# Top-k attention with two expert layers on one core: products with values of two consecutive pairs of heads in one block

## The chip, the cores and the metric

The kernel runs on one core of a Trainium2 chip. The metric is the device time of one execution in microseconds, the median of several runs. Inputs, outputs and all arithmetic seen by the caller are float32.

## The reference

```python
scores = (1 / sqrt(64)) * q @ k.T             # batch 2, 8 heads, 576 rows, head size 64
kth = the 32nd largest score of each row
p = softmax(where(scores >= kth, scores, -1e9))
x = (p @ v), heads side by side               # 1152 x 512
g = domain_probs / sum(domain_probs)          # 1152 x 4
x = sum over 4 experts of g[:, e] * (relu(x @ w1[e]) @ w2[e])        # inner size 1024
out = max(x @ m1, x @ m2, x @ m3) @ mo        # inner size 768
```

## The kernel before

The 1152 rows are nine tiles of 128. A batch has 576 rows, so tile 4 is mixed: its first 64 rows belong to batch 0, the others to batch 1. The work of attention comes in 36 **pairs**: one tile and two heads (`hp`, 0 to 3). Pairs 0 to 15 are tiles 0 to 3; pairs 16 to 23 are tiles 4 and 5 in the order of `MIX`, (4,0), (5,0), (4,1), (5,1), (4,2), (4,3), (5,2), (5,3); pairs 24 to 35 are tiles 6 to 8.

A pair passes through these steps of class `Pair`. PE makes the scores of head j (`scores`, L408); ACT copies them from PSUM to `s` (L432), in buffers with the tags s0 (five of them, `AHEAD_S`) and s1 (four, `S1`). DVE finds the 32 largest of each row with four MAX8 and three MATCH_REPLACE8 (`topk`, L437). ACT and DVE make the masked exponentials `p` (`exp`, `mask`) and their sums. PE turns `p` (`trans_p`, L484): four blocks of 128 columns for each head into one bank, which ACT copies to `pt` (L494), and the 64 columns left over of both heads into another, copied to `pt4` (L499). The two `pt` of a pair have one buffer each. DVE takes the reciprocal of the sums (`rr`, L510), ACT spreads it over 64 columns for each head (`rb`, L514), PE turns that too (`trans_r`, L516, bank `psr`) and ACT copies it to `r` (L521). The product with values (`pv`, L523, bank `psv`) is one full-width matmul with the left-over rows (`v_last`, 128 columns of weights, L533) and eight half-width ones (`vt`, 64 columns of weights, head 0 into partitions 0 to 63 and head 1 into 64 to 127, L536). The matmuls are plain f32 and each appears in a trace as two records. For a mixed tile all of this is done once for each batch, on half of the columns. DVE multiplies the product by `r` into `xt` (`norm`, L540), and `split_x` (L545) makes a high part `xh` on ACT and a low part `xl` on POOL.

The experts' matmuls are f32r: each product is three of them, `xl` by `whi`, `xh` by `whi`, `xh` by `wlo` (L684 to L686). All banks but two come from one ring of six (`bank`).

The order of every engine's instructions is fixed when the program is built. Attention is laid out in slots, eight to a pair, by tables of slot numbers (`FIRST` to `LOOSE`; pairs from 12 on mostly use `BOTH` or `LOOSE`, which put the product with values and the turn of `r` at slot 17 of the pair, that is slot 1 two pairs later). After each slot the planner in the main loop adds work of the experts until a counter of PE's columns (`clock["pe"]`) has reached a goal that grows with DVE's work of that slot. An engine then takes its instructions in that order, each when its semaphores allow it.

Of the kernel before, what the change touches and what calls it, by code (L numbers as in the profile page):

```python
# [10 lines left out]
F32 = mybir.dt.float32  # L11
# [35 lines left out]
EARLY = 7  # L47

# [12 lines left out]
def kernel(  # L61
# [71 lines left out]
    def pe(n):  # L133
        clock["pe"] += n / 2400.0
# [264 lines left out]
    class Pair:  # L399
        def __init__(self, n):  # L400
            self.n = n
            self.c, self.hp, self.t = pairs[n]
            self.s, self.w, self.m, self.nb = {}, {}, {}, {}
            self.p = self.rs = None
            self.pt = {}

            self.did = set()

            self.on_pool = [n in ON_POOL[j] for j in range(2)]
            self.on_act = [n in ON_ACT[j] for j in range(2)]  # L410
# [74 lines left out]
        def trans_p(self, part):  # L485
# [3 lines left out]
            if part < 2:  # L489
                for r in range(NR):  # L490
                    nc.tensor.transpose(ps[:, r * P:(r + 1) * P], self.p[:, part, part * TAIL + r * P:part * TAIL + (r + 1) * P], ident)  # L491
                d = at.tile([P, NR, P], F32, tag="pt%d" % part, bufs=1, name="pt")
                self.pt[part] = d
                return lambda: [nc.scalar.activation(out=d, in_=ps.rearrange("p (r n) -> p r n", r=NR), func=AF.Copy),  # L494
                                self.did.add(("pt", part))]
# [16 lines left out]
        def spread(self):  # L512
            self.rb = at.tile([P, 2, D], F32, tag="rb", bufs=1, name="rb")
            nc.scalar.activation(out=self.rb, in_=self.rr.unsqueeze(2).to_broadcast([P, 2, D]), func=AF.Copy)  # L514

        def trans_r(self):  # L516
            ps = bank("psr")
            pe(260)
            nc.tensor.transpose(ps[:, 0:P], self.rb.rearrange("p a d -> p (a d)"), ident)
            self.r = at.tile([P, P], F32, tag="r", name="r")  # L520
            return lambda: [nc.scalar.activation(out=self.r, in_=ps[:, 0:P], func=AF.Copy), self.did.add("r")]  # L521

        def pv(self):  # L523
            assert {("pt", i) for i in range(3)} <= self.did
            ps = bank("psv")
            pe((NR + 1) * 512)
            if self.t == MIXED:
                parts = [(0, slice(0, TAIL)), (1, slice(TAIL, P))]
            else:
                parts = [(0 if self.t < MIXED else 1, slice(0, P))]  # L530
            for b, cols in parts:
                vs, last = vt[b, self.hp]
                nc.tensor.matmul(ps[:, cols], lhsT=last, rhs=self.pt[2][:, cols], start=True, stop=False)  # L533
                for r in range(NR):
                    for j in range(2):
                        nc.tensor.matmul(ps[j * D:(j + 1) * D, cols], lhsT=vs[:, j * NR + r, :],  # L536
                                         rhs=self.pt[j][:, r, cols], start=False, stop=r == NR - 1)
            self.x = ps

        def norm(self):  # L540
            assert "r" in self.did
            self.xt = xfull[:, self.hp, :] if [self.t] in STAGES else at.tile([P, P], F32, tag="xt", bufs=2 + WAITING, name="xt")
            nc.vector.tensor_tensor(out=self.xt, in0=self.x[:, 0:P], in1=self.r, op=ALU.mult)
# [15 lines left out]
    def attention():  # L559
# [38 lines left out]
        for n, (c, hp, t) in enumerate(pairs):  # L598
# [24 lines left out]
            at_slot(s0 + o["pv"], pr.pv)  # L623
            two(s0 + o.get("turn", o["rec"] + 2), pr.trans_r)
            end = max(o["pv"], o["rec"] + 2) + o["lag"]
            if "norm" in o:
                between.setdefault(s0 + o["norm"], []).append((pr.norm, ()))
            else:
                at_slot(s0 + end + 1, pr.norm)
            two(s0 + o.get("split", end + 2), pr.split_x)  # L630
        last = {}
        for n, p in enumerate(pairs):
            o = options(n)
# [451 lines left out]
```

## Time and profile before

| | us |
|---|---|
| median of 3 runs | 742.99 |
| lowest and highest | 742.87, 744.54 |
| the profiled execution | 743.31 |
| its span, first to last instruction | 740.8 |
| PE busy in the span | 718.4 |
| DVE, ACT, POOL busy | 582.6, 504.9, 474.2 |

The profiled execution's time is 2.5 us longer than its span: that lies before the first and after the last instruction. PE's clock is granted in full throughout (1.00 in every stretch). Attention ends at about 450 us, and what follows is the rest of the experts and the last layer. Matmuls overlap each other in the pipeline, so the time from one start to the next tells what one costs, not its duration.

### The profile page before, as it was taken

To read this page: it belongs to the slowest core of one execution; us is meant where nothing else is said; L and a number is where in the kernel's file an instruction comes from. 1 tells how busy PE (TensorE), PEld (TensorE's weight loads), DVE (VectorE), ACT (ScalarE), POOL (GpSimd) and SP (SyncE) were. 2 spreads that over 40 slices of the span, in tenths; PEclk is the share of its full clock that TensorE was granted. 3 is DMA by queue.
4 is the path that set the end of the run, shared out by engine and by line. 5 is a ranking of instruction groups with operands and counts; after the bars stand their busy time and mean duration, and the time that the engine had idled before them with its cause. 6 is when DMAs were issued, how large, how long until landed. Compare 5 with 4: busy or idle time off the path is not lost.

```text
span 740.8 us, 13773 instructions
## 1 busy us (share of the span) xinstructions
PE 718.4 (97%) x4758; PEld 641.4 (87%) x4758; DVE 582.6 (79%) x1172; ACT 504.9 (68%) x1131; POOL 474.2 (64%) x420
## 2 busy tenths in 40 slices
PE   6799999999999999999999999999999999999998
PEld 4587689888989988898998989999989999998996
DVE  6999989989999899999999983867689783333431
ACT  4668989899977878697878777656657654442531
POOL 2513879679979797777878769756645683442520
PEclk9999999999999999999999999999999999999999
DMA  7584455644646464544545537796988764443501
GB/s 220 179 261 176 135 181 168 174 118 138 202 143 189 114 192 124 169 130 129 155 126 161 154 118 241 247 320 195 310 275 308 234 190 186 160 165 109 191 1 42
DMA packets 56485, 130.15 MB, mean 176 GB/s; under 512 B 9760, under 2 KB 23328, under 8 KB 56416
## 3 DMA queue, kind: packets, MB, share of 16 engines
q1 hardware_dynamic: 48064, 120.69, 52.1%
q10 hardware_dynamic: 8352, 8.59, 3.3%
q8 instruction: 37, 0.61, 0.3%
q14 instruction: 32, 0.26, 0.1%
HBM read 120.60 MB, written 8.65 MB: 174 GB/s over the span
## 4 chain that ended last, share of the span: by engine, by line
PE 69%; DVE 15%; ACT 9%; issue 3%; POOL 2%; DMA 1%; ACTq 0%; POOLq 0%
PE ps L684 17%; PE ps L686 17%; PE ps L685 17%; DVE m L445 7%; DVE work L447 6%; PE psv L536 3%; ACT whi L273 3%; PE pss L425 2%; PE psp L491 2%; POOL wlo L279 2%; PE pso L684 2%; PE psa L769 2%; PE pso L685 2%; PE pso L686 2%; PE pss L420 1%
## 5 line engine op out<-in xcount | busy, mean ns | idle before, releaser
L279 POOL TENSOR_TENSOR wlo<-raw,whi 128x512 fp32r<-128x512 f32 x252 | 327.6, 1329 | 130.1 <-ACT whi L273 122.8
L273 ACT ACTIVATE whi<-raw 128x1024 fp32r<-128x1024 f32 x164 | 170.1, 1057 | 36.5 <-PE ps L686 17.0
L684 PE MATMUL ps<-xl,whi 128*128 128x256 f32 (+1 forms) x584 | 173.5, 297 | 0.4 <-POOL xl L557 0.4
L686 PE MATMUL ps<-xh,wlo 128*128 128x256 f32 (+1 forms) x584 | 170.7, 292 | 0.0
L685 PE MATMUL ps<-xh,whi 128*128 128x256 f32 (+1 forms) x584 | 170.6, 292 | 0.0
L445 DVE MAX8 m<-work 128x8 f32<-128x576 f32 x216 | 155.1, 744 | 0.1
L684 PEld LDWEIGHTS ps<-xl,whi 128*128 128x128 f32 x584 | 110.7, 190 | 1.4 <-POOL xl L557 0.6
L685 PEld LDWEIGHTS ps<-xh,whi 128*128 128x128 f32 x584 | 109.7, 188 | 0.8 <-issue 0.2
L686 PEld LDWEIGHTS ps<-xh,wlo 128*128 128x128 f32 x584 | 109.6, 188 | 0.0
L279 DVE TENSOR_TENSOR wlo<-raw,whi 128x1024 fp32r<-128x1024 f32 x38 | 55.7, 1468 | 68.6 <-ACT whi L273 56.7
L447 DVE MATCH_REPLACE8 work<-m,work 128x576 f32<-128x576 f32 x144 | 106.7, 741 | 0.0
L684 PE MATMUL ps<-wlo,h 128*128 128x512 f32 x224 | 90.8, 405 | 0.6 <-POOL wlo L279 0.6
L686 PE MATMUL ps<-whi,h 128*128 128x512 f32 x224 | 87.8, 392 | 1.3 <-POOL h L821 1.3
L685 PE MATMUL ps<-whi,h 128*128 128x512 f32 x224 | 87.7, 391 | 0.0
L249 POOL TENSOR_TENSOR narrow<-narrow,raw 128x256 int32<-128x256 int32 x48 | 45.0, 940 | 30.7 <-issue 10.2
L432 ACT ACTIVATE s<-pss 128x288 f32<-128x288 f32 x144 | 51.2, 399 | 11.6 <-PE pss L420 11.2
L445 DVE MAX8 m<-s 128x8 f32<-128x576 f32 x72 | 53.8, 747 | 4.5 <-ACT s L432 4.5
L447 DVE MATCH_REPLACE8 work<-m,s 128x576 f32<-128x576 f32 x72 | 53.4, 741 | 0.0
L686 PEld LDWEIGHTS ps<-whi,h 128*128 128x128 f32 x224 | 42.1, 188 | 11.2 <-POOL h L821 1.7
L684 PEld LDWEIGHTS ps<-wlo,h 128*128 128x128 f32 x224 | 42.9, 192 | 8.2 <-POOL wlo L279 1.6
L686 PE MATMUL ps<-x2h,wlo 128*128 128x384 f32 x144 | 48.5, 337 | 0.0
L685 PE MATMUL ps<-x2h,whi 128*128 128x384 f32 x144 | 48.3, 336 | 0.0
(111 smaller groups left out, 1461.2 us busy)
## 6 DMA issues: line engine op xcount, KB each, us to landing
raw<-in_w_dram SPq DMA_DIRECT2D x128, 512.0 KB, 4.1
raw<-narrow SPq DMA_DIRECT2D x36, 512.0 KB, 4.4
raw<-in_m_dram SPq DMA_DIRECT2D x36, 256.0 KB, 5.1
whole<-in_w_dram SPq DMA_DIRECT2D x14, 512.0 KB, 6.2
narrow<-narrow ACTq DMA_DIRECT2D x48, 128.0 KB, 4.4
kraw<-in_k_dram SPq DMA_DIRECT2D x16, 288.0 KB, 4.5
qraw<-in_q_dram SPq DMA_DIRECT2D x48, 64.0 KB, 3.9
raw<-in_mo_dram SPq DMA_DIRECT2D x12, 256.0 KB, 4.7
```

The lines of the kernel that those rows point to most:

```text
L249: nc.gpsimd.tensor_tensor(out=out.bitcast(I32), in0=out.bitcast(I32), in1=last, op=ALU.add)
L273: nc.scalar.activation(out=hi, in_=raw, func=AF.Copy)
L279: on.tensor_tensor(out=lo[:, x], in0=raw[:, x], in1=hi[:, x].bitcast(F32), op=ALU.subtract)
L425: nc.tensor.matmul(ps[:, 0:SH], lhsT=l, rhs=r, start=i == 0, stop=i == len(mm) - 1)
L432: nc.scalar.activation(out=s[:, h, :], in_=halves[h][:, 0:SH], func=AF.Copy)
L445: nc.vector.max(m[:, 8 * r:8 * r + 8], src)
L447: nc.vector.match_replace(out=self.w[j], in_to_replace=m[:, 8 * r:8 * r + 8], in_values=src, imm_value=NEG)
L491: nc.tensor.transpose(ps[:, r * P:(r + 1) * P], self.p[:, part, part * TAIL + r * P:part * TAIL + (r + 1) * P], ident)
L536: nc.tensor.matmul(ps[j * D:(j + 1) * D, cols], lhsT=vs[:, j * NR + r, :], rhs=self.pt[j][:, r, cols], start=False, stop=r == NR - 1)
L684: nc.tensor.matmul(ps, lhsT=lh, rhs=rl, start=first, stop=False)
L685: nc.tensor.matmul(ps, lhsT=lh, rhs=rh, start=False, stop=False)
L686: nc.tensor.matmul(ps, lhsT=ll, rhs=rh, start=False, stop=last)
```

## The change

For twelve pairs (`HELD`) the product with values is not made at the pair's own slot. The pair after it makes both: `pv` puts the two results side by side in one bank, first all matmuls with `v_last` and then all half-width ones, and `trans_r` turns both `rb` into one bank, from which ACT makes two copies. With the two pairs of each couple that is 24 pairs. Until then the held pair's `pt` lie in a buffer of `s0` and one of `s1`, and its `rb` in one of `xt`'s. `norm` and `split_x` of both pairs follow each other at the second one's slots.

```diff
--- before.py
+++ after.py
@@ -45,6 +45,7 @@
 LOOSE = dict(stag=4, new=1, scores=-4, at=(14, 14), pv=17, rec=15, lag=2, sum=0)
 
 EARLY = 7
+HELD = (8, 12, 14, 16, 18, 22, 24, 26, 28, 30, 32, 34)
 
 ALONE_FROM, ALONE_STEP = -8, 4
 LOAD, LOAD_FULL = 11, 9
@@ -405,6 +406,7 @@
             self.pt = {}
 
             self.did = set()
+            self.held = n in HELD
 
             self.on_pool = [n in ON_POOL[j] for j in range(2)]
             self.on_act = [n in ON_ACT[j] for j in range(2)]
@@ -489,7 +491,10 @@
             if part < 2:
                 for r in range(NR):
                     nc.tensor.transpose(ps[:, r * P:(r + 1) * P], self.p[:, part, part * TAIL + r * P:part * TAIL + (r + 1) * P], ident)
-                d = at.tile([P, NR, P], F32, tag="pt%d" % part, bufs=1, name="pt")
+                if self.held:
+                    d = at.tile([P, NR, P], F32, tag="s%d" % part, bufs=(AHEAD_S, S1)[part], name="pt")
+                else:
+                    d = at.tile([P, NR, P], F32, tag="pt%d" % part, bufs=1, name="pt")
                 self.pt[part] = d
                 return lambda: [nc.scalar.activation(out=d, in_=ps.rearrange("p (r n) -> p r n", r=NR), func=AF.Copy),
                                 self.did.add(("pt", part))]
@@ -510,37 +515,49 @@
             nc.vector.reciprocal(out=self.rr, in_=self.rs)
 
         def spread(self):
-            self.rb = at.tile([P, 2, D], F32, tag="rb", bufs=1, name="rb")
+            self.rb = at.tile([P, 2, D], F32, tag="xt", bufs=2 + WAITING, name="rb") if self.held else at.tile([P, 2, D], F32, tag="rb", bufs=1, name="rb")
             nc.scalar.activation(out=self.rb, in_=self.rr.unsqueeze(2).to_broadcast([P, 2, D]), func=AF.Copy)
 
-        def trans_r(self):
+        def trans_r(self, *held):
+            both = [*held, self]
             ps = bank("psr")
-            pe(260)
-            nc.tensor.transpose(ps[:, 0:P], self.rb.rearrange("p a d -> p (a d)"), ident)
-            self.r = at.tile([P, P], F32, tag="r", name="r")
-            return lambda: [nc.scalar.activation(out=self.r, in_=ps[:, 0:P], func=AF.Copy), self.did.add("r")]
-
-        def pv(self):
-            assert {("pt", i) for i in range(3)} <= self.did
+            for i, x in enumerate(both):
+                pe(260)
+                nc.tensor.transpose(ps[:, i * P:(i + 1) * P], x.rb.rearrange("p a d -> p (a d)"), ident)
+                x.r = at.tile([P, P], F32, tag="r", name="r")
+
+            def copy():
+                for i, x in enumerate(both):
+                    nc.scalar.activation(out=x.r, in_=ps[:, i * P:(i + 1) * P], func=AF.Copy)
+                    x.did.add("r")
+            return copy
+
+        def pv(self, *held):
+
+            both = [*held, self]
             ps = bank("psv")
-            pe((NR + 1) * 512)
-            if self.t == MIXED:
-                parts = [(0, slice(0, TAIL)), (1, slice(TAIL, P))]
-            else:
-                parts = [(0 if self.t < MIXED else 1, slice(0, P))]
-            for b, cols in parts:
-                vs, last = vt[b, self.hp]
-                nc.tensor.matmul(ps[:, cols], lhsT=last, rhs=self.pt[2][:, cols], start=True, stop=False)
+            for i, x in enumerate(both):
+                assert {("pt", a) for a in range(3)} <= x.did
+                x.x = ps[:, i * P:(i + 1) * P]
+            pe((NR + 1) * 512 * len(both))
+            uses = []
+            for x in both:
+                if x.t == MIXED:
+                    uses += [(x, 0, slice(0, TAIL)), (x, 1, slice(TAIL, P))]
+                else:
+                    uses += [(x, 0 if x.t < MIXED else 1, slice(0, P))]
+            for i, (x, b, cols) in enumerate(uses):
+                nc.tensor.matmul(x.x[:, cols], lhsT=vt[b, x.hp][1], rhs=x.pt[2][:, cols], start=not i, stop=False)
+            for i, (x, b, cols) in enumerate(uses):
                 for r in range(NR):
                     for j in range(2):
-                        nc.tensor.matmul(ps[j * D:(j + 1) * D, cols], lhsT=vs[:, j * NR + r, :],
-                                         rhs=self.pt[j][:, r, cols], start=False, stop=r == NR - 1)
-            self.x = ps
+                        nc.tensor.matmul(x.x[j * D:(j + 1) * D, cols], lhsT=vt[b, x.hp][0][:, j * NR + r, :],
+                                         rhs=x.pt[j][:, r, cols], start=False, stop=i == len(uses) - 1 and r == NR - 1)
 
         def norm(self):
             assert "r" in self.did
             self.xt = xfull[:, self.hp, :] if [self.t] in STAGES else at.tile([P, P], F32, tag="xt", bufs=2 + WAITING, name="xt")
-            nc.vector.tensor_tensor(out=self.xt, in0=self.x[:, 0:P], in1=self.r, op=ALU.mult)
+            nc.vector.tensor_tensor(out=self.xt, in0=self.x, in1=self.r, op=ALU.mult)
 
         def split_x(self):
             if not room(self.t):
@@ -620,16 +637,21 @@
             at_slot(s0 + o.get("guard", o["rec"] - 1), pr.guard)
             at_slot(s0 + o["rec"], pr.recip)
             at_slot(s0 + o.get("spread", o["rec"] + 1), pr.spread)
-            at_slot(s0 + o["pv"], pr.pv)
-            two(s0 + o.get("turn", o["rec"] + 2), pr.trans_r)
+            if pr.held:
+                continue
+            both = [prs[n - 1], pr] if n - 1 in HELD else [pr]
+            at_slot(s0 + o["pv"], pr.pv, *both[:-1])
+            two(s0 + o.get("turn", o["rec"] + 2), pr.trans_r, *both[:-1])
             end = max(o["pv"], o["rec"] + 2) + o["lag"]
-            if "norm" in o:
-                between.setdefault(s0 + o["norm"], []).append((pr.norm, ()))
-            else:
-                at_slot(s0 + end + 1, pr.norm)
-            two(s0 + o.get("split", end + 2), pr.split_x)
+            for x in both:
+                if "norm" in o:
+                    between.setdefault(s0 + o["norm"], []).append((x.norm, ()))
+                else:
+                    at_slot(s0 + end + 1, x.norm)
+                two(s0 + o.get("split", end + 2), x.split_x)
         last = {}
         for n, p in enumerate(pairs):
+            n += n in HELD
             o = options(n)
             last[p[0:2]] = 8 * n + o.get("last", max(o["pv"], o["rec"] + 2) + 2 * o["lag"] + 2)
         for n in range(len(alone)):
```

The instructions are the same in kind and number on every engine; the order changes. On PE, the products with values of pair 26 (at `v_last_111`) and pair 27 (`v_last_112`) before; `pt_`, `ps_` with a number are the left-over rows of turned p and a bank of the experts' products:

```order
L686 MATMUL ps_4685<-xh,wlo 128x256
L533 MATMUL psv<-pt_4672,v_last_111 128x128
L536 MATMUL psv<-pt,vt 64x128 x8
L519 MATMUL psr<-ident,rb 128x128
L684 MATMUL ps_4763<-wlo,h 128x512
L685 MATMUL ps_4763<-whi,h 128x512
L686 MATMUL ps_4763<-whi,h 128x512
```

A block of one pair stands alone among the experts' f32r products, with its one turn of `rb` behind it. Pair 27, later on PE:

```order
L686 MATMUL ps_4860<-xh,wlo 128x256
L533 MATMUL psv<-pt_4836,v_last_112 128x128
L536 MATMUL psv<-pt,vt 64x128 x8
L519 MATMUL psr<-ident,rb 128x128
L684 MATMUL ps_4941<-xl,whi 128x256
L685 MATMUL ps_4941<-xh,whi 128x256
L686 MATMUL ps_4941<-xh,wlo 128x256
```

The two blocks are 61 rows apart. In the changed kernel both stand at pair 27's place on PE:

```order
L706 MATMUL ps_4880<-xl,whi 128x256
L707 MATMUL ps_4880<-xh,whi 128x256
L708 MATMUL ps_4880<-xh,wlo 128x256
L550 MATMUL psv<-pt_4657,v_last_111 128x128
L550 MATMUL psv<-pt_4833,v_last_112 128x128
L554 MATMUL psv<-pt,vt 64x128 x16
L526 MATMUL psr<-ident,rb 128x128 x2
L706 MATMUL ps_4880<-xl,whi 128x256
```

The two `v_last` matmuls come first, 16 half-width ones follow, and then two turns; at pair 26's old place the experts' products run on.

ACT about the copy of `r` for pair 27 before (`s`: scores, `whi`: a weight's high part, `h`: a hidden layer's, `rs`: the sums):

```order
L432 ACTIVATE s<-pss 128x288 x2
L273 ACTIVATE whi<-raw 128x1024
L826 ACTIVATE h<-ps_4860 128x512
L521 ACTIVATE r<-psr 128x128
L273 ACTIVATE whi<-raw 128x1024
L556 ACTIVATE xh<-xt 128x128
```

And in the changed kernel, for pairs 26 and 27:

```order
L434 ACTIVATE s<-pss 128x288 x2
L531 ACTIVATE r<-psr 128x128 x2
L274 ACTIVATE whi<-raw 128x1024
L573 ACTIVATE xh<-xt 128x128 x2
L848 ACTIVATE h<-ps_4880 128x512
L509 ACTIVATE rs<-rs 128x2
```

The two copies of `r` follow each other directly behind the copies of scores; the rounding of a weight and of a hidden layer, which stood ahead of `r`, come behind it. The two `xh` follow each other too.

## Rows read from the trace of the kernel before

**Rows 1.** the page: span and busy time of each engine

```profile
span 740.8 us, 13773 instructions
...
PE 718.4 (97%) x4758; PEld 641.4 (87%) x4758; DVE 582.6 (79%) x1172; ACT 504.9 (68%) x1131; POOL 474.2 (64%) x420
```

**Rows 2.** the chain of waits, 330 to 345 us: start us, us, what

```profile
332.18 1.33 DVE m L445 x2
...
339.41 0.53 PE pss L425 x2
```

**Rows 3.** the chain by line, 341 to 450 us

```profile
by line: PE ps L684 24.0%; PE ps L686 23.9%; PE ps L685 23.9%; PE psv L536 9.1%; PE psp L491 7.2%; PE pss L425 6.8%; PE psv L533 2.1%; PE psr L519 2.1%; PE psp L496 1.0%
```

**Rows 4.** the chain by line, 450 to 741 us

```profile
by line: PE ps L684 28.2%; PE ps L686 28.1%; PE ps L685 28.0%; PE pso L684 4.3%; PE pso L685 4.3%; PE pso L686 4.2%; PE pst L905 1.4%; PE psv L536 0.2%; DVE ob L975 0.1%; ACT ob L973 0.1%; PE psr L519 0.1%; issue 0.0%
```

**Rows 5.** busy time by stretch: PE, PEld, DVE, ACT, POOL, then clock, DMA

```profile
160.00:240.00 80.00, 78.79 (x611) 71.77 (x610) 79.56 (x166) 69.13 (x165) 72.41 (x64) 1.00 0.57 168
...
258.00:340.00 82.00, 79.68 (x621) 71.99 (x621) 78.73 (x168) 65.20 (x159) 67.23 (x60) 1.00 0.52 154
340.00:450.00 110.00, 110.00 (x838) 99.47 (x838) 100.31 (x215) 88.41 (x208) 82.84 (x73) 1.00 0.46 137
```

**Rows 6.** PE's timeline about pair 15's products: start us, us, what

```profile
201.15 0.38 PE L533 MATMUL psv<-pt,v_last 128*128 128x128 f32 x2
201.47 1.09 PE L536 MATMUL psv<-pt,vt 128*64 128x128 f32 x16
202.49 0.33 PE L519 MATMUL psr<-ident,rb 128*128 128x128 f32 x1
202.57 0.36 PE L684 MATMUL ps<-xl,whi 128*128 128x256 f32 x1
202.78 0.28 PE L685 MATMUL ps<-xh,whi 128*128 128x256 f32 x1
202.90 0.28 PE L686 MATMUL ps<-xh,wlo 128*128 128x256 f32 x1
```

**Rows 7.** the same, a window that begins at 201.86 us

```profile
201.63 0.82 PE L536 MATMUL psv<-pt,vt 128*64 128x128 f32 x12
```

**Rows 8.** the same, a window that begins at 202.28 us

```profile
202.06 0.50 PE L536 MATMUL psv<-pt,vt 128*64 128x128 f32 x6
```

**Rows 9.** PE's timeline, the mixed pair 16

```profile
212.75 0.33 PE L533 MATMUL psv<-pt,v_last 128*128 128x64 f32 x2
213.01 0.69 PE L536 MATMUL psv<-pt,vt 128*64 128x64 f32 x16
213.63 0.43 PE L533 MATMUL psv<-pt,v_last 128*128 128x64 f32 x2
213.99 0.69 PE L536 MATMUL psv<-pt,vt 128*64 128x64 f32 x16
214.61 0.33 PE L519 MATMUL psr<-ident,rb 128*128 128x128 f32 x1
```

**Rows 10.** PE's timeline, turning pair 28's p

```profile
362.06 1.04 PE L491 MATMUL psp<-ident,p 128*128 128x128 f32 x8
362.93 0.27 PE L496 MATMUL psp<-ident,p 128*128 128x128 f32 x1
```

**Rows 11.** PE's timeline, pair 24: its wait in brackets

```profile
314.56 0.49 PE L533 MATMUL psv<-pt,v_last 128*128 128x128 f32 x2 [1.19 <-ACT pt L499]
```

**Rows 12.** DVE's timeline after that wait

```profile
322.78 0.69 DVE L828 SCALAR_TENSOR_TENSOR h<-ps,h 128x512 fp32r<-128x512 f32 x1 [1.14 <-ACT h L826]
```

**Rows 13.** DVE's timeline, pair 28's p

```profile
354.50 0.81 DVE L473 SCALAR_TENSOR_TENSOR p<-s,m,p 128x576 f32<-128x576 f32 x1
```

**Rows 14.** ACT's timeline, the last copy of pair 19's p

```profile
250.02 0.28 ACT L499 ACTIVATE pt<-psp 128x128 f32<-128x128 f32 x1
```

**Rows 15.** PE's timeline, pair 19's products

```profile
250.85 0.38 PE L533 MATMUL psv<-pt,v_last 128*128 128x128 f32 x2
```

**Rows 16.** ACT's timeline, the copy of pair 15's r

```profile
203.83 0.28 ACT L521 ACTIVATE r<-psr 128x128 f32<-128x128 f32 x1
```

## The prediction

> **What bounds the kernel now.** I read the page first: PE is busy for 718.4 of the span's 740.8 us [rows 1]. A busy PE is an average, so I went to the chain of waits, stretch by stretch. From 341 to 450 us every piece of it is PE's [rows 3], and from 450 us to the end all but the last copy out is PE's too [rows 4]. Just before that the chain still passes through DVE (332 us), and comes back to PE at 339.4 us [rows 2]. So a PE instruction that goes away after 339 us shortens the run by its whole length, as long as nothing else is late next. The table by stretch tells where something else is: from 160 to 240 us DVE is busy for 79.56 of 80 us, so there PE has nothing to gain by being quick. From 258 to 340 us DVE is idle for 82.00 - 78.73 = 3.3 us and from 340 to 450 us for 110.00 - 100.31 = 9.7 us [rows 5]. A piece of that idle time is DVE's wait for a hidden layer that PE finished late [rows 12], so there DVE can follow a quicker PE.
>
> **How far PE is behind DVE.** What DVE hands to PE is p. Pair 28's p is written by 354.50 + 0.81 = 355.3 us [rows 13], and PE turns it at 362.06 us [rows 10]: 6.7 us to spare. The tight place is the other one, the product with values, which needs ACT's copy of the turned p. Pair 19's last copy ends at 250.02 + 0.28 = 250.30 us [rows 14], and PE begins at 250.85 us [rows 15]: 0.55 us to spare.
>
> **What one joined product saves.** No instruction is added or removed; the counts on all five engines stay. What goes is time between matmuls. A single block, pair 15's [rows 6], in start-to-start times:
> - Its two full-width records (v_last) take 201.47 - 201.15 = 0.32 us. Eight records of full-width f32 transposes stand 362.93 - 362.06 = 0.87 us apart, 0.11 each [rows 10], so two should take 0.22. The other 0.10 us is the change to half-width matmuls.
> - Its 16 half-width records start two by two, in eight steps, and take 202.49 - 201.47 = 1.02 us. In the middle, one window shows twelve records from 201.63 us on [rows 7] and a later one the six from 202.06 us on [rows 8]: so four steps take 0.43 us, 0.11 each. Eight of them make 0.87, so the two ends cost 0.15 us.
> - The turn of r stands 0.08 us before the next product, which itself stands 202.78 - 202.57 = 0.21 us before its successor, where 202.90 - 202.78 = 0.12 us is usual. Leaving costs 0.09 us.
>
> Two blocks joined pay these once: 0.10 + 0.15 + 0.09 = 0.34 us saved. The second turn of r now follows another turn, 0.11 us against 0.08, so 0.31 us remain for each couple.
>
> Two of the twelve couples hold a mixed pair, 16 and 18. Its two batches are two full blocks today [rows 9]: the second one takes 213.99 - 213.63 = 0.36 and 214.61 - 213.99 = 0.62, together 0.98 us. With half the columns a v_last record should take half of 0.11. The eight steps of the first, 213.63 - 213.01 = 0.62 us, are 0.15 of ends and 0.47 of work. The change issues all v_last first and then all half-width records, so the second batch costs 0.11 + 0.47 = 0.58 us: another 0.40 us saved. In sum PE sheds 10 x 0.31 + 2 x 0.71 = 4.5 us.
>
> **Where the savings lie.**
> - Five couples (26 with 27, up to 34 with 35) lie where the chain is PE's alone: 5 x 0.31 = 1.55 us, counted whole. Their cover would be DVE, whose 9.7 idle us and the 6.7 us of spare p leave room.
> - Two couples (22 with 23, 24 with 25) lie between 288 and 329 us, where DVE's waits are for PE: 0.62 us, counted whole.
> - Pair 24's product waits 1.19 us for a copy of p [rows 11], and 8 us later DVE waits 1.14 us for a hidden layer [rows 12]. The order puts products of the experts where this product stood, so the wait goes. The joined block comes 13 us later and asks for pair 25's copy, which may be late in turn. Bounds 0 and 1.19 us; I take the middle, 0.6.
> - The other five couples (8, 12, 14, 16, 18 with their neighbours) hold 3 x 0.31 + 2 x 0.71 = 2.35 us, and DVE is full there. PE can only use up what it has to spare at the products, 0.55 us at pair 19 [rows 15]. Bounds 0 and 2.35; I take the near row, 0.5 us.
>
> Together 1.55 + 0.62 + 0.6 + 0.5 = 3.3 us. The profiled execution took 743.31 us (span 740.8 and 2.5 around it), so 740.0; the median of the runs, 742.99, is 0.3 lower, and I give 739.8 us against it.
>
> **What I cost at nothing.** The first pair's turned p sits a pair longer in a buffer of the scores. Three tiles in two pairs now go round five (four) buffers, but the scores that take a buffer over come after its last reader in every turn of the ring, so the cover is a whole pair of DVE's work; gone, it would cost ACT's copies of scores and then DVE. The even pair's x comes a pair later (the products of pairs 19 and 24 begin 314.56 - 250.85 = 63.7 us apart, 12.7 for one) [rows 11, 15], but a stage begins with the odd one. The odd x comes later by the longer block: two records 0.22, eight steps 0.87 and a turn 0.11, so 1.20 us. Covers: ACT copies pair 15's r at 203.83 us [rows 16], 203.83 - 202.82 = 1.01 us after its turn ended [rows 6]. That is almost all of it. At some couples, 26 with 27 among them, the planner now puts the rounding of a weight and of a hidden layer behind r where they stood ahead of it, so ACT comes to r sooner and waits the more; what covers that is ACT's own idle time, 110.00 - 88.41 = 21.6 us from 340 to 450 us [rows 5], some 4 us for each couple. In SP's queue a few loads change places by one, and the first loads of the second layer's weights, which go into the scores' buffers, now come behind the last joined product, which ends 1.20 us after today's. Bounds 0 and 1.20 us; I take 0, since no load is in the chain after 450 us [rows 4].
>
> **The rivals.**
> - DVE is the bound after all. PE's gain then turns into waits for copies of p, and only the five couples in PE's own chain count, 1.55 us: 741.4 us, in a band from 740.8 to 742.6. For it: 79.56 of 80 us. Against it: the 13 idle us after 258 us.
> - The change doesn't save on PE at all: the long gaps belong to the matmuls and not to a change of width. Then only pair 24's wait goes: 742.4 us. Against it stand the rows above, full-width records 0.11 us apart where no half-width one follows. The Trainium skill ("TensorE: Matmul & The Clock Gate", Back-to-back issue gap) has a rule of this kind: in a stream of weight loads and matmuls each matmul's spacing follows from its own columns, some 81 ns for 128 of them, whatever its neighbours. By that rule the joined blocks save nothing. The trace does not agree with it: records of 128 columns stand 0.11 or 0.21 us apart, as the next is of the same width or not.
> - All of it counts: 4.5 us and pair 24's 1.19, so 743.0 - 5.7 = 737.3 us. For it: PE is the chain's largest part. Against it: the full DVE before 240 us.
> - Slower: ACT reaches the copy of the odd pair's r before the longer block is through. It waits 1.20 - 1.01 = 0.19 us, and the copy of the even pair's r, 0.28 us [rows 16], now stands ahead of it; behind both stand the copies of scores for which DVE waits. Twelve couples x 0.47 = 5.6 us on a full DVE, against the 2.2 us (1.55 + 0.62) that PE sheds after 288 us: 743.0 + 5.6 - 2.2 = 746.4 us. It decides where ACT's turn comes sooner than 1.2 us after the turn of r. Against it: PE comes to the block earlier by what it has shed so far, and from the second couple on (2 x 0.31) that is more than 0.19 us.
>
> **How the numbers follow.** My forecast, 738.5 to 740.7 us, 0.47; all of it counts, 0.08; DVE bound, 0.25; no saving on PE, 0.05; slower, 0.15, more than its price alone would get, since the order takes cover away from r at several couples. A measurement of this kernel can tell about 0.3% (2.2 us) from no change, so faster means below 740.8 us: 0.47 + 0.08 = 0.55. Same: 0.25 + 0.05 = 0.30. Slower by over 0.3%, 745.2 us or more: 0.15. For eight in ten the range takes in the forecast, the DVE band, the case without savings and part of the full sum: 737.8 to 743.6 us. It leaves out the slower case and the rest of the full one.
>
> **What would show it.** Right: v_last records in fours, half-width records in 32s, a joined block of some 2.6 us against 2 x 1.42 (from 201.15 to 202.57 us today); no wait of PE before pair 24's old place; the chain after 339 us still PE's alone; attention's last product some 3 us earlier, and the rest of the program as long as before. Wrong: PE idle before joined products, waiting for a copy of p (DVE bound); a joined block of 2.84 us (no saving); DVE waiting for xt's r or ACT for the turn of r (slower).

## The result and the profile after

The changed kernel takes 749.0 us in the median of five runs (747.66, 748.92, 749.00, 749.91 and one of 761.22); the kernel before took 743.31 us in the same comparison. The ratio is 1.0073, with an interval of 1.0058 to 1.0089: slower, and above the whole range that I gave. Five of the kernels below have two groups of times, 5 to 8 us apart (the kernel before has not, in twenty runs from 742.0 to 747.4); where that is so, the text names both groups and compares the lower ones. The profiled execution took 748.92 us.

The page of the changed kernel: span, busy time of each engine, and the chain that ended last, by engine:

```profile
span 746.8 us, 13785 instructions
...
PE 718.9 (96%) x4758; PEld 643.3 (86%) x4758; DVE 582.5 (78%) x1172; ACT 506.9 (68%) x1131; POOL 476.1 (64%) x420
...
PE 53%; DVE 26%; ACT 14%; issue 4%; POOL 2%; DMA 1%; SPq 0%; ACTq 0%; POOLq 0%; DVEq 0%
```

The chain of the kernel before:

```profile
PE 69%; DVE 15%; ACT 9%; issue 3%; POOL 2%; DMA 1%; ACTq 0%; POOLq 0%
```

The busy times are within 2 us of those of before [rows 1], the span is 6.0 us longer. The chain that ended last went 15% through DVE before and now goes 26%. Busy time by stretch, the columns as in [rows 5]:

```profile
160.00:240.00 80.00, 76.67 (x595) 70.19 (x596) 76.82 (x160) 68.70 (x165) 70.57 (x63) 1.00 0.56 164
258.00:340.00 82.00, 80.26 (x638) 73.42 (x637) 78.69 (x171) 67.01 (x161) 62.94 (x56) 1.00 0.48 148
340.00:450.00 110.00, 108.00 (x796) 98.40 (x795) 102.05 (x215) 84.32 (x200) 82.21 (x72) 0.98 0.45 140
383.00:386.60 3.60, 3.60 (x34) 3.27 (x34) 3.60 (x10) 2.87 (x9) 0.73 (x1) 0.53 0.02 5
```

DVE, full from 160 to 240 us before (79.56 of 80), is now idle for 3.2 us there. From 340 to 450 us PE, which had never been idle, is idle for 2.0 us, and its clock is at its lower level, 1.2 of 2.4 GHz, for most of 383 to 386.6 us (mean 0.53).

The saving itself came. PE's timeline at couple 30 with 31, to be held against [rows 6]:

```profile
409.51 0.61 PE L550 MATMUL psv<-pt,v_last 128*128 128x128 f32 x4
410.05 1.97 PE L554 MATMUL psv<-pt,vt 128*64 128x128 f32 x32
411.95 0.44 PE L526 MATMUL psr<-ident,rb 128*128 128x128 f32 x2
412.14 0.48 PE L706 MATMUL ps<-wlo,h 128*128 128x512 f32 x1
```

From the first v_last to the next product it takes 412.14 - 409.51 = 2.63 us; a single block took 202.57 - 201.15 = 1.42 [rows 6], two of them 2.84. With one slow spacing less behind the block (0.09) that is 0.30 us a couple. PE's busy time from 45 to 460 us, before and now:

```profile
45.00:460.00 415.00, 407.82 (x3069) 359.99 (x3068) 383.03 (x816) 342.31 (x821) 319.81 (x283) 1.00 0.53 158
```

```profile
45.00:460.00 415.00, 401.35 (x3025) 355.67 (x3026) 380.46 (x811) 338.57 (x813) 315.69 (x276) 1.00 0.50 153
```

PE stands idle for 415.00 - 401.35 = 13.65 us, where it stood for 7.18. So about two thirds of what was lost, the 6.0 us and the 4 us and more that PE saved, are stops of PE. Some 1.6 us are a slow clock (below); the rest lies in smaller delays that were not followed. Two places show how the stops come about.

**At 122 us**, where pair 8's block used to stand before. First the changed kernel (PE, POOL, ACT), then the kernel before (PE, POOL); in brackets the idle time ahead of an instruction and what ended it:

```profile
121.92 0.50 PE L708 MATMUL ps<-whi,h 128*128 128x512 f32 x1 [1.74 <-POOL h L843]
...
120.59 1.28 POOL L843 TENSOR_TENSOR h<-raw,h 128x512 fp32r<-128x512 f32 x1
...
126.86 1.09 ACT L499 ACTIVATE pt<-psp 128x512 f32<-128x512 f32 x2 [2.73 <-PE psp L493]
```

```profile
122.18 0.40 PE L686 MATMUL ps<-whi,h 128*128 128x512 f32 x1
...
120.54 1.29 POOL L821 TENSOR_TENSOR h<-raw,h 128x512 fp32r<-128x512 f32 x1
```

POOL has h ready at 121.83 us before and at 121.87 now. Before, PE came to the product that reads it at 122.18 us, with 0.35 us to spare; without the block it comes early and waits 1.74 us. Pair 9's turning of p stands behind it, with products pulled ahead of it as well, and its last record comes at 127.10 us instead of 125.36. ACT idles for 2.73 us until that turning. DVE has two new stops, 1.41 us at 126.43 us for one of the pulled products and 1.57 us at 133.57 us for ACT's copy of scores, and its idle time from 116 to 160 us grows from 4.4 to 7.2 us.

**At 370 to 387 us**, couple 28 with 29. The changed kernel's DVE, ACT and PE:

```profile
372.94 0.69 DVE L850 SCALAR_TENSOR_TENSOR h<-ps,h 128x512 fp32r<-128x512 f32 x1 [2.33 <-ACT h L848]
373.55 0.08 DVE L449 MATCH_VALUE_LOAD work<-m,work 128x8 f32 x1
373.62 0.74 DVE L449 MATCH_REPLACE8 work<-m,work 128x576 f32<-128x576 f32 x1
374.28 1.83 DVE L475 SCALAR_TENSOR_TENSOR p<-s,m,p 128x576 f32<-128x576 f32 x1
...
381.04 0.31 ACT L519 ACTIVATE rb<-rr 128x128 f32<-128x128 f32 x1 [3.42 <-DVE rr L515]
381.26 1.07 ACT L499 ACTIVATE pt<-psp 128x512 f32<-128x512 f32 x2
...
381.89 0.49 PE L550 MATMUL psv<-pt,v_last 128*128 128x128 f32 x2 [1.58 <-ACT pt L499]
382.55 0.49 PE L550 MATMUL psv<-pt,v_last 128*128 128x128 f32 x2 [0.17 <-ACT pt L504]
382.96 3.56 PE L554 MATMUL psv<-pt,vt 128*64 128x128 f32 x32
```

The kernel before, DVE at the same place:

```profile
368.40 0.74 DVE L447 MATCH_REPLACE8 work<-m,work 128x576 f32<-128x576 f32 x1
369.06 1.59 DVE L473 SCALAR_TENSOR_TENSOR p<-s,m,p 128x576 f32<-128x576 f32 x1
...
370.87 0.69 DVE L828 SCALAR_TENSOR_TENSOR h<-ps,h 128x512 fp32r<-128x512 f32 x1 [0.21 <-ACT h L826]
```

The hidden layer's instruction stood behind the last match-replace and p; now it stands ahead of them. DVE and ACT are already some 2.2 us later here than before. ACT comes to its part at 372.32 us (370.24 before), no later than that; but DVE is at the instruction sooner in its order, so it waits 2.33 us with attention's work ready behind it. Everything that follows is in order: DVE's reciprocal is late, ACT waits 3.42 us for it with the turned p of pair 29 ready, the copies stand behind that wait, PE stands 1.75 us before the joined block, and in the block the clock is at its lower level: 386.45 - 382.96 = 3.49 us for the 32 half-width records, which took 411.95 - 410.05 = 1.90 us at the next couple.

### The profile page after: what moved, and what is told of

Its sections match the earlier page's. It is cut to its first block, busy times and chain, and to the rows that moved or that the text cites. A ratio compares the mean times of both kernels' runs of the same rounds, so it can differ in the third digit from the quotient of the medians.

```text
span 746.8 us, 13785 instructions
## 1 busy us (share of the span) xinstructions
PE 718.9 (96%) x4758; PEld 643.3 (86%) x4758; DVE 582.5 (78%) x1172; ACT 506.9 (68%) x1131; POOL 476.1 (64%) x420
## 4 chain that ended last, share of the span: by engine, by line
PE 53%; DVE 26%; ACT 14%; issue 4%; POOL 2%; DMA 1%; SPq 0%; ACTq 0%; POOLq 0%; DVEq 0%
PE ps L708 13%; PE ps L706 13%; PE ps L707 13%; DVE m L447 11%; DVE work L449 10%; ACT whi L274 4%; PE psv L554 2%; ACT pt L499 2%; PE pso L706 2%; DVE h L850 2%; PE psa L791 2%; PE pso L707 2%; PE pso L708 2%; DVE p L475 2%; PE pss L422 1%
## 5 line engine op out<-in xcount | busy, mean ns | idle before, releaser
L280 POOL TENSOR_TENSOR wlo<-raw,whi 128x512 fp32r<-128x512 f32 x252 | 331.3, 1346 | 129.1 <-ACT whi L274 118.1
L850 DVE SCALAR_TENSOR_TENSOR h<-ps,h 128x512 fp32r<-128x512 f32 x46 | 31.4, 682 | 22.3 <-ACT h L848 20.6
```

The costliest lines, as they stand in the source:

```text
L280: on.tensor_tensor(out=lo[:, x], in0=raw[:, x], in1=hi[:, x].bitcast(F32), op=ALU.subtract)
L850: lambda: [nc.vector.scalar_tensor_tensor(out=hl[:, g], in0=ps, scalar=0.0, in1=hh[:, g].bitcast(F32), op0=ALU.max, op1=ALU.subtract) for ...
```

## Experiments

My theory after these two places (A): the planner counts PE's columns for the joined block only when it is reached, so at the second pair of each couple it has pulled two groups of products (3072 columns; 6144 at one couple) ahead of the turning of p, on every engine, and that order does the harm. Its rivals: the block's absence alone uncovers waits (A2), the tiles held in other buffers (B), the longer block and ACT's r (C).

**No pair held.** `HELD = ()` in the changed kernel; the new order of a mixed pair's matmuls stays.

> No pair is held; what stays of the change is that a mixed pair's two v_last matmuls both go ahead of its half-width ones (4 pairs, about 0.28 us of TensorE each, 2.017 to 1.742 at pair 20). Every theory that puts the loss on held pairs expects 741.5 to 743.5 us, and no wait of TensorE at 122 us. If it comes out at 745 or more, the loss has nothing to do with holding pairs.

743.03 us, ratio 1.0004 (0.9995 to 1.0012). The loss belongs to held pairs.

**The tiles alone.**

```diff
-            if pr.held:
-                continue
-            both = [prs[n - 1], pr] if n - 1 in HELD else [pr]
+            both = [pr]
...
-            n += n in HELD
```

> Only the tiles: turned p of the 12 first pairs in the scores' buffers and their rb in x's buffers, every product at its own slot and unjoined. Theory B (these tiles make VectorE's scores or ScalarE wait for buffers): 744.5 us or more. Otherwise, as argued in the prediction: the time of the kernel with no pair held, 742.5 to 743.5 us.

742.71 us, ratio 0.9996 (0.9985 to 1.0006). Theory B falls.

**The clock charged at the held pair's own slot.** All twelve couples are joined; only the planner's counter differs, and with it the order.

```diff
             if pr.held:
+                at_slot(s0 + o["pv"], pe, (NR + 1) * 512)
+                at_slot(s0 + o.get("turn", o["rec"] + 2), pe, 260)
                 continue
...
-            pe((NR + 1) * 512 * len(both))
+            pe((NR + 1) * 512)
...
+            pe(260)
             for i, x in enumerate(both):
-                pe(260)
```

> All 12 couples joined as in the change, but the planner's TensorE clock is charged for the held pair's product at that pair's own slot, so that the experts' products stand at every odd pair's turning of p exactly where they stood before (in the change they stand 3072 columns, two groups of products, further ahead there, for one couple 6144). Theory A (products pulled ahead of the odd pair's turning make TensorE wait in order and deliver that turning late): the 1.74 us wait at 122 us may stay in part, but the odd turnings come within 0.5 us of before, and the joined blocks' savings show: 739 to 741.5 us. Theory A2 (the block's absence alone uncovers waits, wherever products stand): 745 to 749. Theory B (tiles held in the scores' and x's buffers) and theory C (longer block, ACT waiting at r): 747 to 750, since both are unchanged.

Eight runs from 743.02 to 744.11 us (middle 743.6), four from 750.0 to 751.2; over all a ratio of 1.0042 (1.0016 to 1.0068). The lower group is 5.4 us under the changed kernel, so the order is most of the loss. But my 739 to 741.5 us failed: what PE saves still does not arrive. PE stands idle for 9.44 us from 45 to 460 us (7.18 before, 13.65 in the changed kernel). DVE's 2.33 us wait is gone. At the two places above, these stops of PE are left; the longest of the others that are new or longer are for ACT's copies of scores (1.26 us at 221.5 us) and of p (1.05 at 300.4):

```profile
121.92 0.49 PE L710 MATMUL ps<-whi,h 128*128 128x512 f32 x1 [1.24 <-POOL h L845]
...
377.10 0.49 PE L550 MATMUL psv<-pt,v_last 128*128 128x128 f32 x2 [0.54 <-ACT pt L499]
377.75 0.49 PE L550 MATMUL psv<-pt,v_last 128*128 128x128 f32 x2 [0.16 <-ACT pt L504]
```

**The pulled order alone.** No pair held or joined; `pe(...)` in `pv` and `trans_r` is multiplied by 0 for the twelve first pairs and by 2 for their successors.

> No pair is held or joined; alone the planner's TensorE clock is charged as in the change: nothing at the first pair of each couple, double at the second. So the experts' products are pulled ahead of the odd pairs' turnings of p by the same 3072 columns (6144 for one couple) as in the change, while every block stays where it was. Theory A (the pulled order itself does the harm, on all engines: VectorE and ScalarE come in order to hidden layers whose products TensorE has not done): slower by 3 to 6 us, 746 to 749 us. Theory A2 (the blocks' absence is what uncovers waits; the order alone is harmless) and theory B (tiles held in the scores' buffers): 742.5 to 744 us.

749.5 us, ratio 1.0084 (1.0070 to 1.0099). Nothing is moved but the experts' work, and it costs as much as the whole change. The same cascade stands in its trace (DVE, ACT, PE, and the stretch behind it):

```profile
375.09 0.69 DVE L852 SCALAR_TENSOR_TENSOR h<-ps,h 128x512 fp32r<-128x512 f32 x1 [2.24 <-ACT h L850]
...
383.38 0.31 ACT L521 ACTIVATE rb<-rr 128x128 f32<-128x128 f32 x1 [2.48 <-DVE rr L517]
...
384.88 0.49 PE L552 MATMUL psv<-pt,v_last 128*128 128x128 f32 x2 [1.41 <-ACT pt L506]
...
386.00:389.00 3.00, 3.00 (x29) 2.70 (x25) 3.00 (x8) 3.00 (x9) 0.74 (x1) 1.00 0.02 5
```

**Held, but not joined.** First with the changed kernel's order:

```diff
-            at_slot(s0 + o["pv"], pr.pv, *both[:-1])
-            two(s0 + o.get("turn", o["rec"] + 2), pr.trans_r, *both[:-1])
+            for x in both:
+                at_slot(s0 + o["pv"], x.pv)
+                two(s0 + o.get("turn", o["rec"] + 2), x.trans_r)
```

> The first pair of each couple is held as in the change (same buffers, same slot, same order of products), but the two pairs do their products and their turns of r in banks of their own, one after the other: what is lost is the saving of joining (12 couples x about 0.3 us, 3.6 us, and some 0.5 more in the mixed couples). Theory A and theory B: as slow as the change or slower, 749 to 753 us. Theory C (the joined block, with its one evacuation for two, makes ACT and the odd x wait): back to 743 to 746 us, since the first pair's r and x no longer wait for the second's.

750.29 us (five runs, 750.03 to 753.68 and one of 767.69), ratio 1.0111 (1.0094 to 1.0128): theory C falls, since two short blocks are no quicker than a long one. Then the same with the clock charged at the own slot, as above:

> Held and moved to the odd pair's slot but not joined, with the clock charged at the own slot: against the joined kernel with that charge (743.6 us in most of its runs, 12 joined couples) it lacks only the saving of joining. If moving the first pair's product costs what joining saves, so that the two cancel: 746.5 to 748.5 us. If the saving does not count since other engines set the pace: 743.3 to 744.8 us.

Two runs at 746.8 us and four from 753.1 to 753.7; over all 1.0106 (1.0072 to 1.0140). In the lower groups, here only two of six runs, moving the first pair's product costs 746.8 - 743.0 = 3.8 us even where the products' order is kept (A2, the smaller part), and joining gives 746.8 - 743.6 = 3.2 us back.

**Some couples only.** `HELD` from 22 on; then all but 28.

> Held only 22, 24, 26, 28, 30, 32, 34; the five early couples stay single. If the loss is made where DVE is full (the early couples, 1.7 to 3.6 us late by 210 us in the change's trace) and the late couples bring what I forecast for them: 740 to 741.5 us. If the 1.58 us wait before couple 28 with 29 and the clock's fall behind it recur, 3.3 us are lost there: 743 to 745. If the loss belongs to every couple alike: 746 to 747.

746.45 us, ratio 1.0060 (1.0033 to 1.0088), against 740 to 741.5 if the early couples made the loss. So about 3.4 of the 6 us arise among the late couples, where I had counted the saving whole; the stop of 1.58 us at couple 28 with 29 is there again, to the hundredth, though without the slow clock behind it. The time would also fit a loss at every couple alike (746 to 747 us); the next kernel speaks against that.

> The change with pair 28 not held. In the change's trace the turning of pair 30 comes 3.8 us later against before than that of pair 29: TensorE waits 1.75 us at the joined block of 28 and 29 and its clock is at half for 3.4 us behind it (1.7 us lost). If that cascade is this couple's own, both go and the time is 745 to 746 us. If the slack that the pulled order eats is common to the neighbours, the wait moves to another couple: 747 to 749 us.

745.04 us, ratio 1.0033 (1.0008 to 1.0059). Without that couple the wait and the slow clock are gone from the profile, and 4 of the 6 us with them.

**ACT's spread of rr behind the copies of turned p.** The copies stood behind DVE's reciprocal; in pairs with the loose table the spread now comes a slot later.

```diff
-            at_slot(s0 + o.get("spread", o["rec"] + 1), pr.spread)
+            at_slot(s0 + o.get("spread", o["rec"] + 1 + (o is LOOSE)), pr.spread)
```

Three kernels have it: the one charged at the own slot, the one without held pairs, and the change as it is.

> As the run charged at the own slot, and besides ScalarE's spread of rr into rb stands one slot later in the loosely staged pairs, behind the copies of turned p, so that these copies no longer stand behind VectorE's reciprocal (in the run charged at the own slot ScalarE idled 3.42 us before rb at 376.25 us, with the turned p of pair 29 ready, and TensorE then waited 0.54 and 0.16 us for these copies). If those copies are what the joined blocks wait for, TensorE's waits for copies of p (0.36, 0.81, 1.05, 0.54, 0.16 us in that run) shrink by half or more and it comes to 740.5 to 742.5 us. If VectorE's pace sets the time whatever the order on ScalarE: 743 to 744.5. If rb now comes late to the turn of r: 744 or more, with TensorE waiting before psr.

> The control of the run before: no pair held, and the spread of rr a slot later in the same pairs. It takes from the unjoined kernel its waits for copies of p (1.19 us at 314.56 and 0.98 us at 339.41 in the trace of before). If joining saves anything in the end, this one is slower than the joined one by 1 to 3 us: 741.5 to 743.5 us. If it is as fast as the joined one, the joined products' saving does not reach the end of the program even without those waits.

> The change as it is, with only the spread of rr a slot later. If the pulled order does its harm by way of ScalarE, whose copies of turned p stand behind a reciprocal that VectorE delivers late (3.42 us of idle before rb at 381.04 in the change's trace), most of the loss goes: 741 to 744 us, no wait at the block of 28 and 29. If the harm is made by VectorE's own wait for a hidden layer (2.33 us at 372.94 there), the spread takes only what it takes from the unjoined kernel, 4.3 us: 744 to 746 us.

The first: six runs from 737.9 to 739.9 us, six from 743.7 to 745.8; over all a ratio of 0.9974 (0.9949 to 0.9999). The second: eight from 738.1 to 739.2, four from 743.6 to 744.1; over all a ratio of 0.9960 (0.9939 to 0.9980). So a line that has nothing to do with joining takes over 4 us off the unjoined kernel in the lower group, more than joining was ever to bring; my forecast of 741.5 to 743.5 was too high, and neither group of the first lies in the 740.5 to 742.5 us that I gave. Of the first kernel's stops of PE for copies of p (five, from 0.16 to 1.05 us, without the late spread) one is left in its profile, 0.36 us at 146.7 us. And all twelve couples joined are no faster than none (738.3 against 738.6). The third: four runs from 742.5 to 744.6, five from 751.3 to 753.0; over all 1.0064 (1.0025 to 1.0104). In its profile (744.56 us; DVE, ACT, PE) DVE's wait is still there, but PE's stop at couple 28 with 29 is not, since ACT makes the copies first; a stop of 1.54 us comes 10 us later instead:

```profile
371.49 0.69 DVE L850 SCALAR_TENSOR_TENSOR h<-ps,h 128x512 fp32r<-128x512 f32 x1 [2.20 <-ACT h L848]
...
375.86 1.09 ACT L499 ACTIVATE pt<-psp 128x512 f32<-128x512 f32 x2
...
379.40 0.31 ACT L519 ACTIVATE rb<-rr 128x128 f32<-128x128 f32 x1 [2.28 <-DVE rr L515]
...
378.81 0.61 PE L550 MATMUL psv<-pt,v_last 128*128 128x128 f32 x4
```

The lower group's middle, 744.1 us, is 4.9 us under the changed kernel, hardly more than the 4.4 us that the same line takes from the kernel without held pairs. So it doesn't decide whether the pulled order harms by way of ACT's copies or of DVE's own wait.

**All three together:** late couples only, clock charged at the own slot, late spread.

> Only the seven late couples are joined (22 with 23 up to 34 with 35), the planner's clock is charged at the held pair's own slot, and the spread of rr stands one slot later. In the run with that spread and no held pair TensorE has no wait of 0.15 us or more after 185 us, so there what a joined block saves (0.30 us, measured) should reach the end in full: 738.6 - 7 x 0.30 = 736.5, so 736 to 737.5 us where no VectorE instruction is held up. If joining pays nothing even there (VectorE, or copies that come late to the joined block, set the pace): 738 to 740 us.

All six runs lie from 736.8 to 738.6 us; the median is 737.15, ratio 0.9921 (0.9904 to 0.9937): faster than both kernels. Busy time by stretch, in it and then in the kernel with the late spread and no pair held:

```profile
190.00:340.00 150.00, 150.00 (x1186) 137.63 (x1185) 146.11 (x311) 126.54 (x303) 128.25 (x112) 1.00 0.54 159
340.00:450.00 110.00, 110.00 (x841) 100.79 (x840) 97.75 (x210) 87.00 (x202) 89.26 (x78) 1.00 0.49 148
```

```profile
190.00:340.00 150.00, 149.98 (x1195) 137.11 (x1194) 145.83 (x311) 126.75 (x304) 128.15 (x112) 1.00 0.53 159
340.00:450.00 110.00, 110.00 (x825) 99.52 (x824) 98.69 (x210) 85.72 (x200) 87.13 (x76) 1.00 0.46 141
```

From 190 to 450 us PE hardly stands in either, and here joining pays: 1.3 us in the spans (736.1 and 734.8), 1.5 against the lower group (738.6 and 737.15), of the 2.1 expected. Product by product, each removed block takes 1.42 us and 0.08 behind it, and each joined one adds 1.21, so 0.29 us a couple; the missing 0.7 us is lost in steps of a few hundredths between the couples.

**Two of these kernels once more,** those that fell into the upper group most often:

> One more look at the change with the late spread, whose runs fell into two groups (742.5 to 744.6, and 751.3 to 753.0 us at a mean clock of 0.993 to 0.995). If a run of the upper group is what the late-spread joined kernel showed in its profile (one masking instruction of VectorE, p<-s,m,p, of 6.42 us behind four roundings of weights on GpSimd, where others take 0.8 to 2.0, and TensorE's clock at half after it), a profile above 750 us shows such an instruction of 5 us or more. If it is only the clock, no VectorE instruction of that line is over 2.1 us.

> One more look at the held, unjoined kernel with the charge at the own slot (746.8 us in two runs, 753.1 to 753.7 in four, at a clock of 0.997 to 0.998). The same question: a profile at 753 us shows one masking instruction of VectorE of 5 us or more (it is held up by GpSimd), or none over 2.1 us (another cause).

One run each: 742.25 and 746.59 us, both in the lower group, so they tell nothing about the upper one. Against the first profile of its kernel, the first one does tell something about the clock (last section).

## Why the prediction was wrong

**What PE saves: right.** I took 0.31 us for a couple; it is 0.30. For couple 16 with 17 I took 0.71 and it is 0.48: from the first v_last to the next product 214.69 - 212.75 = 1.94 and 227.20 - 225.78 = 1.42 us before, 231.74 - 228.77 = 2.97 now, and 0.09 behind the block. I had v_last records of 64 columns at half of 0.11 us; the first two stand 0.055 apart, but the others 0.11, like those of 128. In exchange pairs 20 and 21, which I left out, gained some 0.3 us each. (My four terms, taken from 742.99, make 739.7 us, not 739.8.)

**The step that failed** is in "Where the savings lie": "The order puts products of the experts where this product stood, so the wait goes." I took this as a gain of 0.6 us at one pair, and gave the order no price anywhere else, though the same step happens at all twelve couples; the only things that I saw change places, ACT's roundings about r and a few loads, I put at nothing. Pair 24's wait did go, but a few us later, at 328.53 us, PE stands 1.30 us for POOL's h, which it did not before. For the order moves on every engine, and an instruction of the experts that comes earlier in DVE's queue blocks attention behind it when ACT or PE has not got that far. Alone it costs 6.4 us (749.5 against 743.1), and with the joined blocks undoing it gives back 5.4.

**"Counted whole"** for the five couples after 339 us failed with it. I looked for slack at p (6.7 us) and in DVE's idle time, not at what ACT's copies of the odd pair's p stand behind: DVE's reciprocal. The rows for it were there in the trace of before (ACT, PE), at pair 29:

```profile
376.69 0.31 ACT L514 ACTIVATE rb<-rr 128x128 f32<-128x128 f32 x1 [1.53 <-DVE rr L510]
376.90 1.07 ACT L494 ACTIVATE pt<-psp 128x512 f32<-128x512 f32 x2
...
378.19 0.49 PE L533 MATMUL psv<-pt,v_last 128*128 128x128 f32 x2
```

The cover of the copies was a reciprocal in time, not p in time: ACT waits for DVE's reciprocal, copies, and PE's product follows the last copy (377.86 + 0.28 = 378.14 us) with nothing to spare.

**Bounds "0 and 2.35"** for the five early couples had no end below nothing. A product is also cover: PE reached the product at 122.18 us only 0.35 us after POOL's h, and taking 1.42 us of PE's work from ahead of it had to make PE wait over a microsecond, as it did (1.24 us with the old order, 1.74 with the pulled one).

**Tiles, at nothing: right** (742.71 us). **ACT at r, my slower rival: wrong.** The side was right, its mechanism was not: two separate blocks are as slow (750.29), and the stops at r that it asks for are hardly there: from 100 to 450 us DVE stands 0.56 us ahead of xt before and 0.25 now, and ACT ahead of its copy of r 1.2 and 1.6, 1.05 of it behind the slow block of couple 28 with 29. Only at the last couple they are longer (ACT 2.84 us for 0.99, DVE 4.73 for 3.14), and from 460 us on PE is busy throughout. **DVE bound:** in the kernel with the old order the waits return all that is saved (743.6 against 743.0), as that rival has it for the early couples, but copies of p do it among the late ones too (1.05 us at 300.4 us, 0.54 at 377.1). **No saving on PE:** refuted by the 0.30 us.

Not settled: which of the pulled instructions at the early couples costs how much, what part of the loss runs by way of ACT, and what makes the upper groups of times. Only kernels charged at the own slot or with the late spread have them, so they may belong to these orders; the comparisons of lower groups leave that cost out.

## What to carry to other kernels

Where a program's order is fixed by a planner that counts an engine's time, moving one block reorders every queue: compare the orders on all engines, and price what comes earlier at its place by what it must wait for. A block that goes away was also cover for the instruction behind it; read that instruction's slack to its releaser first. And before making an engine quicker, look at what its waits stand behind: here one late spread on ACT was worth more (4.4 us in the lower groups) than twelve joined products.

## What the runs showed of the hardware

The length of a stop alone does not tell whether TensorE's clock falls behind it. In the changed kernel the clock was at its lower level for some 3.4 us behind stops of 1.58 and 0.17 us. In the kernel with late couples only, the same stops stand at the same couple, and the block behind them is at the higher level (1.00 from 383 to 390 us):

```profile
383.15 0.49 PE L550 MATMUL psv<-pt,v_last 128*128 128x128 f32 x2 [1.58 <-ACT pt L499]
383.80 0.49 PE L550 MATMUL psv<-pt,v_last 128*128 128x128 f32 x2 [0.17 <-ACT pt L504]
384.22 1.97 PE L554 MATMUL psv<-pt,vt 128*64 128x128 f32 x32
```

So the slow clock is no fixed part of that stop's price. The change with the late spread was profiled twice (744.56 and 742.25 us). In both, PE stops for 2.00 us until 186.9 us; the stretch behind it, in the first and in the second:

```profile
187.30:190.70 3.40, 3.40 (x19) 3.40 (x18) 3.20 (x8) 3.40 (x9) 3.40 (x4) 0.50 0.75 241
```

```profile
187.30:190.70 3.40, 3.40 (x32) 3.40 (x30) 3.21 (x8) 3.40 (x9) 3.40 (x4) 1.00 0.80 267
```

The next turning of p begins at 201.29 us in the first and at 199.67 in the second, and the spans are 742.5 and 740.2 us: so two executions of one kernel can differ by most of 2 us through one fall of the clock. Stops of 1.41 us in the kernel with the pulled order alone (1.00 from 386 to 389 us) and of 1.19 us at pair 24 before [rows 11] had no fall behind them.

The clock's first rise varies too. PE is not at the higher level throughout, as I had it ahead of the prediction: in the kernel before, sixteen half-width records at 25.72 us take 1.98 us, where they take 1.09 at 201.47 [rows 6], although the profile reads 1.00 at both places. In most profiles the records are quick by 36 us (42 to 44 of them from 36 to 40 us). In those of the kernel held apart and of the late couples there are 16 and 17, and by 70 us both are over 3 us late, ahead of the first held pair. That fits what sets these two profiled executions (753.68 and 749.13 us) above the middle of their kernels' runs (750.29 and 746.45).

In the late-spread kernel with all couples joined, the profile (744.28 us, upper group) holds one masking instruction of DVE that took 6.42 us, where the other 23 take 0.8 to 1.9. DVE and POOL at that place, and the stretch behind it:

```profile
266.96 6.42 DVE L475 SCALAR_TENSOR_TENSOR p<-s,m,p 128x576 f32<-128x576 f32 x1
...
267.73 5.04 POOL L280 TENSOR_TENSOR wlo<-raw,whi 128x512 fp32r<-128x512 f32 x4
...
275.00:285.00 10.00, 7.52 (x55) 6.27 (x56) 9.65 (x23) 8.57 (x22) 6.15 (x6) 0.66 0.42 140
```

It ends at 273.38 us, 0.6 us after POOL's four roundings (272.77), which ran at 1.26 us each, less than the mean of that line in the whole run, 1.35. By these times all four of POOL's went ahead of DVE's one. In the joined kernel without the late spread POOL's roundings begin at 269.95 us, after this instruction, and it took 0.81 us. PE ran dry, and its clock was at 0.66 in the mean from 275 to 285 us. The Trainium skill ("GPSIMD Engine Reference", Key points) says that GpSimd shares its SBUF interfaces with VectorE, with contention where a VectorE instruction has two SBUF inputs, as this one has (s and p). The trace agrees with that, and 6.42 against 0.8 us would be a price of 5.6 us on one instruction; no run here isolates it. That this is what makes the upper groups of the other kernels is a guess that no run here shows.
